# K tiles loaded further ahead of V tiles, and the gate folded into the attention weights, in a one-core decode kernel

## The chip, the core and the metric

The kernel runs on one core of one Trainium2 chip. The metric is the device time of one execution in microseconds (us); 0.2% of it is about 5 us. A core has a matmul engine (TensorE, in the profile PE, with its weight loads PEld), a vector engine (VectorE, DVE), a scalar engine (ScalarE, ACT), GpSimd (POOL) and SyncE (SP), whose queue issues every DMA of this kernel. A DMA is spread over 16 DMA engines.

## The reference

One token (a row `x` of 512 numbers) passes through attention over a cached K and V of 32 heads, 65,536 positions and 128 numbers per position, and through a small gated feed-forward block; a scalar gate mixes the two. All inputs are bf16.

```python
def reference(A_x, A_k_cache, A_v_cache, A_wq, A_wo, B_x, B_w_gate, B_w_up, B_w_down, gate_w):
    x = A_x
    g = sigmoid((x * gate_w).sum(-1, keepdims=True))      # one scalar
    q = (x @ A_wq).reshape(1, 1, 32, 128)                 # heads moved ahead of positions
    scores = einsum("bhqd,bhkd->bhqk", q, A_k_cache) * (128 ** -0.5)
    p = softmax(scores, axis=-1)
    o = einsum("bhqk,bhkd->bhqd", p, A_v_cache)
    a = o.reshape(1, 1, 4096) @ A_wo
    b = (silu(x @ B_w_gate) * (x @ B_w_up)) @ B_w_down
    return g * a + (1 - g) * b
```

K and V are 512 MB each, so nearly all bytes that the kernel reads (1,087.64 MB by the profile) are these two.

## The kernel before

**Tiles.** A tile of K or V holds 16,384 positions: 128 partitions of 128 positions, 4 MB. A head has G = 4 tiles of each, so N = 128 tiles of K and 128 of V. They share one ring of five buffers of 4 MB (`SLOTS`, line 17; pool `ring`); the weights `wq_t`, `gu_t` and `wd_t` pass through the same ring at the start. A load that needs a buffer waits on SP's queue until the last reader of an old tile is done, and all later loads wait behind it, since that queue is in order.

**A K tile** (`products`, line 197, and `scores`, line 216). DVE multiplies the tile by the query, copied to all partitions (line 207), and then folds 128 numbers per position down to 16 with three adds of halves (line 211). PE sums the last 16 with an identity matrix in 16 accumulated matmuls (line 221) into the head's score tile `S_ps` in PSUM. The K buffer is free after those.

**A V tile** (`values`, line 252). PE makes 32 matmuls, four positions of each partition at a time: `P_sb` (the exponentials) is the weight, V the moving operand, and a 4 x 512 tile `O_ps` accumulates over a head (line 258). The V buffer is free after those. The diagonal blocks of `O_ps` add up to the head's output.

**Between the two**, once per head: DVE takes the row maximum of the scores (`row_max`, line 230); ACT spreads it on a diagonal (line 235); PE makes it visible to all partitions (line 237); DVE takes the maximum over that (`top`, line 242); ACT makes the exponentials and their row sums (line 246). After the head's last V tile, `head_out` (line 267) copies `O_ps` to SBUF on ACT, PE sums the row sums over partitions (line 271) and collects the four diagonal blocks (line 275); `project` (line 284) takes the reciprocal of the sum, multiplies the head's output by it on DVE (lines 286 and 287) and adds its part of the output projection to `a_ps` (line 288), with rows of A_wo that `load_wo` (line 138) brings in for four heads at a time.

**Order.** Each engine runs its instructions in the order in which the program issues them. The loop at line 296 runs n over 132 steps. Step n loads K tile n and V tile n - 4, so that V runs four tiles behind K. In a step that begins a head, DVE's work on the K tile is cut into two halves, and the row maximum, `top` and the reciprocal of earlier heads are woven between the halves (lines 306 to 315). The feed-forward block is worked in steps 1 to 3. After the loop comes the last head's `head_out` and `project`, then `diff` = a - b (line 332), `out_sb` = diff * g + b (line 334) and the store (line 338).

Of the kernel before, what the change touches and what calls it, by code (L numbers as in the profile page):

```python
# [8 lines left out]
ACT = mybir.ActivationFunctionType  # L9
ALU = mybir.AluOpType  # L10
AXIS = mybir.AxisListType
P = 128
# [3 lines left out]
NB = 128  # L16
SLOTS = 5

WIDTH = 16


@with_exitstack
def kernel(
# [14 lines left out]
    nc = tc.nc  # L38
    bf16 = mybir.dt.bfloat16
    f32 = mybir.dt.float32  # L40

    _, H, Sk, Dh = A_k_cache.shape
    D = A_x.shape[2]
# [3 lines left out]
    G = Sk // (NB * P)  # L47
    NBH = Sk // P
    N = H * G
    QG = 4  # L50
    assert Dh == P and Sk % (NB * P) == 0 and NBH <= 512 and H % QG == 0 and G >= 2
    scale = float(Dh) ** -0.5

    consts = ctx.enter_context(tc.tile_pool(name="consts", bufs=1))
    ring = ctx.enter_context(tc.tile_pool(name="ring", bufs=SLOTS))
    small = ctx.enter_context(tc.tile_pool(name="small", bufs=2))
    wo_pool = ctx.enter_context(tc.tile_pool(name="wo_pool", bufs=2))
    psum_s = ctx.enter_context(tc.tile_pool(name="psum_s", bufs=2, space=bass.MemoryType.PSUM))
    psum_o = ctx.enter_context(tc.tile_pool(name="psum_o", bufs=2, space=bass.MemoryType.PSUM))
    psum_a = ctx.enter_context(tc.tile_pool(name="psum_a", bufs=1, space=bass.MemoryType.PSUM))  # L60
    psum_m = ctx.enter_context(tc.tile_pool(name="psum_m", bufs=2, space=bass.MemoryType.PSUM))
# [20 lines left out]
    ones_f = consts.tile([P, P], f32, name="ones_f")  # L82
# [6 lines left out]

    rowsum = consts.tile([P, H], f32, name="rowsum")  # L90
    oT = consts.tile([P, H], bf16, name="oT")
    gval = consts.tile([1, 1], f32, name="gval")
    b_sb = consts.tile([1, D], f32, name="b_sb")
    a_ps = psum_a.tile([1, D], f32, name="a_ps")

    K_tiles, V_tiles, S_tiles, P_tiles, O_tiles = {}, {}, {}, {}, {}
# [38 lines left out]
    WG = 4  # L135
    wo_tiles = {}

    def load_wo(g):
        wo_tiles[g] = wo_pool.tile([P, WG, D], bf16, name="wo_sb")
        rows = A_wo[g * WG * P : (g + 1) * WG * P, :]  # L140
        nc.sync.dma_start(out=wo_tiles[g], in_=rows.rearrange("(h p) n -> p h n", p=P))
# [20 lines left out]
        nc.scalar.activation(out=eg, in_=gu_sb[:, :FT], func=ACT.Exp, scale=-1.0)  # L162
        return gu_sb, eg

    def feed_forward_out(gu_sb, eg):
        nc.vector.tensor_scalar_add(eg, eg, 1.0)
        nc.vector.reciprocal(eg, eg)
        hprod = consts.tile([P, FT], f32, name="hprod")
        nc.vector.tensor_tensor(out=hprod, in0=gu_sb[:, :FT], in1=eg, op=ALU.mult)
        hT = consts.tile([P, FT], bf16, name="hT")  # L170
        nc.vector.tensor_tensor(out=hT, in0=hprod, in1=gu_sb[:, FT:], op=ALU.mult)
        xg = consts.tile([P, KT], f32, name="xg")
        nc.vector.tensor_tensor(out=xg, in0=xT, in1=gwT, op=ALU.mult)
        xs = consts.tile([P, 1], f32, name="xs")
        nc.vector.tensor_reduce(out=xs, in_=xg, axis=AXIS.X, op=ALU.add)
        b_ps = psum_m.tile([1, D], f32, name="b_ps", tag="misc")
        for ft in range(FT):
            nc.tensor.matmul(
                b_ps,
                lhsT=hT[:, ft : ft + 1],  # L180
                rhs=wd_sb[:, ft, :],
                start=(ft == 0),
                stop=(ft == FT - 1),
            )
        nc.scalar.activation(out=b_sb, in_=b_ps, func=ACT.Copy)
        g_ps = psum_m.tile([1, 1], f32, name="g_ps", tag="misc")
        nc.tensor.matmul(g_ps, lhsT=xs, rhs=ones_f[:, 0:1], start=True, stop=True)
        eg2 = consts.tile([1, 1], f32, name="eg2")
        nc.scalar.activation(out=eg2, in_=g_ps, func=ACT.Exp, scale=-1.0)
        return eg2  # L190

    def gate(eg2):
        nc.vector.tensor_scalar_add(eg2, eg2, 1.0)
        nc.vector.reciprocal(gval, eg2)


    def products(n, a, b):

        h = n // G
        K = K_tiles[n][:, a:b, :]  # L200
        qb = q_bc[:, h * Dh : (h + 1) * Dh]
        q_rep = bass.AP(
            tensor=qb.tensor,
            offset=qb.offset,
            ap=[list(qb.ap[0]), [0, b - a], [1, Dh]],
        )
        yield nc.vector.tensor_tensor(out=K, in0=K, in1=q_rep, op=ALU.mult)  # L207
        half = Dh
        while half > WIDTH:
            half //= 2  # L210
            yield nc.vector.tensor_tensor(  # L211
                out=K[:, :, 0:half], in0=K[:, :, 0:half], in1=K[:, :, half : 2 * half],
                op=ALU.add,
            )
# [15 lines left out]
    def row_max(h):  # L230

        m = small.tile([P, 1], f32, name="m")
        nc.vector.tensor_reduce(out=m, in_=S_tiles[h], axis=AXIS.X, op=ALU.max)  # L233
        diag = small.tile([P, P], f32, name="diag")
        nc.scalar.activation(out=diag, in_=ident_f, func=ACT.Copy, scale=m)  # L235
        mT_ps = psum_m.tile([P, P], f32, name="mT_ps", tag="misc")
        nc.tensor.matmul(mT_ps, lhsT=ones_f, rhs=diag, start=True, stop=True)  # L237
        return mT_ps

    def exponentials(h, mT_ps):  # L240
        top = small.tile([P, 1], f32, name="top")
        nc.vector.tensor_reduce(out=top, in_=mT_ps, axis=AXIS.X, op=ALU.max)  # L242
        bias = small.tile([P, 1], f32, name="bias")
        nc.scalar.activation(out=bias, in_=top, func=ACT.Copy, scale=-scale)  # L244
        P_tiles[h] = small.tile([P, NBH], bf16, name="P_sb")
        nc.scalar.activation(  # L246
            out=P_tiles[h], in_=S_tiles[h], func=ACT.Exp, bias=bias, scale=scale,
            accum_out=rowsum[:, h : h + 1],
        )
        del S_tiles[h]  # L250

    def values(n):

# [10 lines left out]
            )  # L264
        del V_tiles[n]

    def head_out(h):
        O_sb = small.tile([4, 4 * Dh], f32, name="O_sb")
        nc.scalar.activation(out=O_sb, in_=O_tiles.pop(h), func=ACT.Copy)  # L269
        oh_ps = psum_m.tile([P, 2], f32, name="oh_ps", tag="misc")  # L270
        nc.tensor.matmul(  # L271
            oh_ps[:, 1:2], lhsT=ones_f, rhs=rowsum[:, h : h + 1], start=True, stop=True
        )
        for c in range(4):
            nc.tensor.matmul(  # L275
                oh_ps[:, 0:1],
                lhsT=O_sb[:, c * Dh : (c + 1) * Dh],
                rhs=ident_f[0:4, c : c + 1],
                start=(c == 0),
                stop=(c == 3),  # L280
            )
        return oh_ps

    def project(h, oh_ps):
        recip = small.tile([P, 1], f32, name="recip")
        nc.vector.reciprocal(recip, oh_ps[:, 1:2])  # L286
        nc.vector.tensor_tensor(out=oT[:, h : h + 1], in0=oh_ps[:, 0:1], in1=recip, op=ALU.mult)  # L287
        nc.tensor.matmul(  # L288
            a_ps,
            lhsT=oT[:, h : h + 1],  # L290
            rhs=wo_tiles[h // WG][:, h % WG, :],
            start=(h == 0), stop=(h == H - 1),
        )

    ff = None
    for n in range(N + G):
        h, g = divmod(n, G)
        v = n - G
        if g == 0 and h % WG == 2 and h // WG + 1 < H // WG:
            load_wo(h // WG + 1)  # L300
        if n < N and n > 1:
            load(K_tiles, A_k_cache, n, "K_t")
        if v >= 0:
            load(V_tiles, A_v_cache, v, "V_t", (0, NB) if v < N - 1 else (0, 64, 96, 112, NB))
        vector = products(n, 0, NB) if n < N else iter(())
        if g == 0 and h > 0:
            if n < N:
                vector = (i for a in (0, NB // 2) for i in products(n, a, a + NB // 2))
            next(vector, None)
            mT_ps = row_max(h - 1)  # L310
            next(vector, None)
            exponentials(h - 1, mT_ps)
            if h > 1:
                oh_ps = head_out(h - 2)
                next(vector, None)
                project(h - 2, oh_ps)
        if n == 1:
            ff = feed_forward_in()
        if n == 2:
            ff = feed_forward_out(*ff)  # L320
        if n == 3:
            gate(ff)
        for _ in vector:
            pass
        if v >= 0:
            values(v)
        if n < N:
            scores(n)
    project(H - 1, head_out(H - 1))

    diff = consts.tile([1, D], f32, name="diff")
    nc.vector.tensor_tensor(out=diff, in0=a_ps, in1=b_sb, op=ALU.subtract)  # L332
    out_sb = consts.tile([1, D], bf16, name="out_sb")
    nc.vector.scalar_tensor_tensor(  # L334
        out=out_sb, in0=diff, scalar=gval[0:1, 0:1], in1=b_sb,
        op0=ALU.mult, op1=ALU.add,
    )
    nc.sync.dma_start(out=out[0], in_=out_sb)


# [28 lines left out]
```

## Time and profile before

| what | value |
|---|---|
| median of 3 runs (lowest to highest) | 2556.45 us (2555.84 to 2557.48) |
| the profiled execution's own time | 2556.5 us |
| its span, first to last instruction | 2554.7 us |
| bytes moved, mean rate over the span | 1088.61 MB, 426 GB/s |
| DMA engines, share of the span (main queue) | 99.2% |
| DVE busy | 2173.4 us (85%) |
| PE busy, weight loads beside it | 1738.5 us (68%), 717.3 us (28%) |
| ACT busy | 66.8 us (3%) |
| mean granted TensorE clock (1 is full speed) | 0.754 |

The profile takes one execution apart. "Busy" is the time in which an engine executes; "idle before" in a group's or a timeline's line is how long the engine sat before the instruction, with what released it behind an arrow. The granted clock is the share of full speed that TensorE was allowed at the time. The time of the run is 1.8 us above the span; that part lies around the instructions, and I carry it over unchanged.

### The profile page before, as it was taken

The page shows a single profiled execution, that of the slowest core. Times are in us where ns is not written, and L with a number is a line of the kernel's source. Part 1 is how long each engine was busy: PE and PEld are TensorE (multiplying, and loading weights), DVE is VectorE, ACT ScalarE, POOL GpSimd, SP SyncE. Part 2 cuts the span into 40 slices and gives each one's busy share as a digit, 9 for nine tenths or more (in the row PEclk, how much of TensorE's full clock was granted, in tenths as well). Part 3 has the DMA queues.
Part 4 walks back from the last instruction along what each step waited for, and adds up shares of the span by engine and source line. Part 5 has one row for each costly group of instructions (what it writes and reads, how often), then busy time and mean ns, then how long its engine had stood idle before and what let it go on. Part 6 is the DMA issues. An engine that isn't in the chain of part 4 may idle for free.

```text
span 2554.7 us, 15161 instructions
## 1 busy us (share of the span) xinstructions
PE 1738.5 (68%) x6720; PEld 717.3 (28%) x6720; DVE 2173.4 (85%) x779; ACT 66.8 (3%) x174; POOL 0.7 (0%) x6
## 2 busy tenths in 40 slices
PE   3477666766776676667666776677666667766677
PEld 2232222322232222222222232222222222322233
DVE  6998888888988888888888888888888888888982
ACT  1000000000000000000000000000000000000000
POOL 0000000000000000000000000000000000000000
PEclk7677777777777777777777777777777777777778
DMA  9999999999999999999999999999999999999996
GB/s 407 434 426 433 430 431 430 429 432 430 432 429 431 429 432 429 430 431 429 432 429 431 428 433 429 432 428 433 429 431 431 428 432 430 431 430 432 430 431 278
DMA packets 42451, 1088.61 MB, mean 426 GB/s; under 512 B 4625, under 2 KB 8722, under 8 KB 8978
## 3 DMA queue, kind: packets, MB, share of 16 engines
q1 hardware_dynamic: 42386, 1087.66, 99.2%
q8 instruction: 52, 0.85, 0.1%
q14 instruction: 13, 0.11, 0.0%
HBM read 1087.64 MB, written 0.00 MB: 426 GB/s over the span
## 4 chain that ended last, share of the span: by engine, by line
DMA 72%; PE 24%; DVE 3%; issue 0%; ACT 0%; SPq 0%; DVEq 0%
DMA V_t<-in_A_v_cache_dram 70%; PE O_ps L258 23%; DVE K_t L207 2%; DVE K_t L211 1%; DMA K_t<-in_A_k_cache_dram 1%; DMA wq_t<-in_A_wq_dram 0%; PE qg_ps L113 0%; PE S_ps L221 0%; PE oh_ps L275 0%; DVE m L233 0%; ACT O_sb L269 0%; PE a_ps L288 0%; ACT P_sb L246 0%; DVE out_sb L334 0%; DVE diff L332 0%
## 5 line engine op out<-in xcount | busy, mean ns | idle before, releaser
L258 PE MATMUL O_ps<-V_t,P_sb 128*4 128x512 bf16 x4096 | 1157.0, 452 | 544.1 <-DMA V_t<-in_A_v_cache_dram 541.9
L207 DVE TENSOR_TENSOR K_t<-K_t,q_bc 128x16384 bf16<-128x16384 bf16 (+1 forms) x159 | 1116.9, 7025 | 249.3 <-DMA K_t<-in_A_k_cache_dram 243.8
L211 DVE TENSOR_TENSOR K_t<-K_t 128x2048 bf16<-128x2048 bf16 (+3 forms) x477 | 1030.0, 2159 | 13.2
L258 PEld LDWEIGHTS <-P_sb 128*4 128x4 bf16 x4096 | 397.3, 97 | 1298.0 <-issue 955.1
L221 PE MATMUL S_ps<-K_t,ident_b 128*128 128x128 bf16 x2048 | 466.0, 394 | 71.0 <-DVE K_t L211 61.3
L221 PEld LDWEIGHTS <-ident_b 128*128 128x128 bf16 x2048 | 223.1, 114 | 308.1 <-issue 110.2
L275 PE MATMUL oh_ps<-ident_f,O_sb 4*128 4x1 f32 x256 | 58.8, 346 | 76.5 <-ACT O_sb L269 76.5
L286 DVE RECIPROCAL recip<-oh_ps 128x1 f32<-128x1 f32 x32 | 5.4, 168 | 105.1 <-PE oh_ps L275 105.1
L237 PE MATMUL mT_ps<-diag,ones_f 128*128 128x128 f32 x64 | 24.9, 490 | 92.3 <-ACT diag L235 92.3
L275 PEld LDWEIGHTS oh_ps<-ident_f,O_sb 4*128 4x128 f32 x256 | 56.1, 319 | 79.2 <-ACT O_sb L269 76.6
L235 ACT ACTIVATE diag<-ident_f,m 128x128 f32<-128x128 f32 x32 | 12.9, 402 | 2327.3 <-DVE m L233 2327.3
L237 PEld LDWEIGHTS mT_ps<-diag,ones_f 128*128 128x128 f32 x64 | 15.6, 304 | 108.0 <-ACT diag L235 108.0
L288 PE MATMUL a_ps<-wo_sb,oT 128*1 128x512 bf16 x32 | 18.5, 580 | 14.6 <-DVE oT L287 14.6
L233 DVE TENSOR_REDUCE m<-S_ps 128x1 f32<-128x512 f32 x32 | 21.8, 683 | 6.5 <-PE S_ps L221 6.5
L246 ACT ACTIVATE P_sb<-S_ps,bias 128x512 bf16<-128x512 f32 x32 | 22.0, 687 | 1.0
L269 ACT ACTIVATE O_sb<-O_ps 4x512 f32<-4x512 f32 x32 | 18.2, 570 | 32.0 <-PE O_ps L258 32.0
L113 PE MATMUL qg_ps<-wq_t,X_bc 128*128 128x512 bf16 x32 | 8.4, 428 | 14.1 <-DMA wq_t<-in_A_wq_dram 14.1
L271 PEld LDWEIGHTS oh_ps<-rowsum,ones_f 128*128 128x128 f32 x64 | 16.8, 321 | 0.4 <-issue 0.4
L271 PE MATMUL oh_ps<-rowsum,ones_f 128*128 128x1 f32 x64 | 13.3, 278 | 0.0
L242 DVE TENSOR_REDUCE top<-mT_ps 128x1 f32<-128x128 f32 x32 | 9.0, 282 | 1.0 <-PE mT_ps L237 1.0
L113 PEld LDWEIGHTS <-X_bc 128*128 128x128 bf16 x32 | 3.5, 108 | 18.5 <-issue 13.0
L244 ACT ACTIVATE bias<-top 128x1 f32<-128x1 f32 x32 | 6.5, 203 | 62.8 <-DVE top L242 62.8
(34 smaller groups left out, 46.3 us busy)
## 6 DMA issues: line engine op xcount, KB each, us to landing
K_t<-in_A_k_cache_dram SPq DMA_DIRECT2D x128, 4096.0 KB, 35.5
V_t<-in_A_v_cache_dram SPq DMA_DIRECT2D x127, 4096.0 KB, 29.4
wq_t<-in_A_wq_dram SPq DMA_DIRECT2D x1, 4096.0 KB, 12.4
wo_sb<-in_A_wo_dram SPq DMA_DIRECT2D x8, 512.0 KB, 30.1
V_t<-in_A_v_cache_dram SPq DMA_DIRECT2D x1, 2048.0 KB, 24.4
gu_t<-in_B_w_gate_dram SPq DMA_DIRECT2D x1, 1792.0 KB, 34.7
gu_t<-in_B_w_up_dram SPq DMA_DIRECT2D x1, 1792.0 KB, 38.4
wd_t<-in_B_w_down_dram SPq DMA_DIRECT2D x1, 1792.0 KB, 42.2
```

Source lines behind the costliest of these rows:

```text
L207: yield nc.vector.tensor_tensor(out=K, in0=K, in1=q_rep, op=ALU.mult)
L211: yield nc.vector.tensor_tensor(out=K[:, :, 0:half], in0=K[:, :, 0:half], in1=K[:, :, half : 2 * half], op=ALU.add,)
L221: nc.tensor.matmul(S_tiles[h][:, g * NB : (g + 1) * NB], lhsT=ident_b, rhs=K_tiles[n][:, :, c], start=(c == 0), stop=(c == WIDTH - 1),)
L233: nc.vector.tensor_reduce(out=m, in_=S_tiles[h], axis=AXIS.X, op=ALU.max)
L235: nc.scalar.activation(out=diag, in_=ident_f, func=ACT.Copy, scale=m)
L237: nc.tensor.matmul(mT_ps, lhsT=ones_f, rhs=diag, start=True, stop=True)
L246: nc.scalar.activation(out=P_tiles[h], in_=S_tiles[h], func=ACT.Exp, bias=bias, scale=scale, accum_out=rowsum[:, h : h + 1],)
L258: nc.tensor.matmul(O_tiles[h], lhsT=P_tiles[h][:, g * NB + j : g * NB + j + 4], rhs=V_tiles[n][:, j : j + 4, :], start=(g == 0 and j == 0) ...
L269: nc.scalar.activation(out=O_sb, in_=O_tiles.pop(h), func=ACT.Copy)
L271: nc.tensor.matmul(oh_ps[:, 1:2], lhsT=ones_f, rhs=rowsum[:, h : h + 1], start=True, stop=True)
L275: nc.tensor.matmul(oh_ps[:, 0:1], lhsT=O_sb[:, c * Dh : (c + 1) * Dh], rhs=ident_f[0:4, c : c + 1], start=(c == 0), stop=(c == 3),)
L288: nc.tensor.matmul(a_ps, lhsT=oT[:, h : h + 1], rhs=wo_tiles[h // WG][:, h % WG, :], start=(h == 0), stop=(h == H - 1),)
```

## The change

It does five things.

1. The loop runs over a list of steps. V starts at step 5 instead of 4, so K is five tiles ahead. From step 40 on, each step with n % 4 == 3 loads no V while V is less than eight tiles behind; that happens at n = 43, 47 and 51, after which K is eight tiles ahead. After the last K come eight steps with V alone (before: four).
2. `products` is issued whole in every step. The row maximum follows it on DVE. The rest of the softmax (`spread`, `exponentials`, and a new `total`) is issued after the step's `values` and `scores`. `P_sb` has a pool of its own with three buffers instead of two.
3. The sum of the row sums over partitions moves from `head_out` to `total`, right behind the exponentials. Two steps into the next head, `weight` on DVE makes gate / sum, one factor per head (`rg`). `head_out` then scales with that factor on ACT.
4. The gate is computed on all partitions. (1 - gate) * b is made in step 3 and opens the accumulation in `a_ps` with a matmul against a single 1, so the end is one copy from `a_ps` to `out_sb`. The feed-forward's middle part now comes behind `products(2)` on DVE instead of ahead of it.
5. In the last `head_out`, ACT and DVE each copy one half of `O_ps`. `load_wo` goes by V's tile number: with V tiles 8, 24, 40, ... .

```diff
+LAG = 8
+SPREAD = 40
+    ppool = ctx.enter_context(tc.tile_pool(name="ppool", bufs=3))
...
-    def feed_forward_out(gu_sb, eg):
+    def feed_forward_mid(gu_sb, eg):
...
-        nc.scalar.activation(out=b_sb, in_=b_ps, func=ACT.Copy)
-        g_ps = psum_m.tile([1, 1], f32, name="g_ps", tag="misc")
-        nc.tensor.matmul(g_ps, lhsT=xs, rhs=ones_f[:, 0:1], start=True, stop=True)
+        g_ps = psum_m.tile([P, 1], f32, name="g_ps", tag="misc")
+        nc.tensor.matmul(g_ps, lhsT=ones_f, rhs=xs, start=True, stop=True)
...
+    def feed_forward_out(b_ps, eg2):
         nc.vector.tensor_scalar_add(eg2, eg2, 1.0)
         nc.vector.reciprocal(gval, eg2)
+        rest = consts.tile([1, 1], f32, name="rest")
+        nc.vector.tensor_scalar(
+            out=rest, in0=gval[0:1, :], scalar1=-1.0, scalar2=1.0, op0=ALU.mult, op1=ALU.add
+        )
+        nc.scalar.activation(out=b_sb, in_=b_ps, func=ACT.Copy, scale=rest)
+        nc.tensor.matmul(a_ps, lhsT=ones_f[0:1, 0:1], rhs=b_sb, start=True, stop=False)
...
+    def total(h):
+        tot_ps = psum_m.tile([P, 1], f32, name="tot_ps", tag="misc")
+        nc.tensor.matmul(tot_ps, lhsT=ones_f, rhs=rowsum[:, h : h + 1], start=True, stop=True)
+        return tot_ps
+
+    def weight(h, tot_ps):
+        recip = small.tile([P, 1], f32, name="recip")
+        nc.vector.reciprocal(recip, tot_ps)
+        nc.vector.tensor_tensor(out=rg[:, h : h + 1], in0=recip, in1=gval, op=ALU.mult)
...
-    def head_out(h):
+    def head_out(h, last=False):
         O_sb = small.tile([4, 4 * Dh], f32, name="O_sb")
-        nc.scalar.activation(out=O_sb, in_=O_tiles.pop(h), func=ACT.Copy)
...
+        cut = 2 * Dh if last else 4 * Dh
+        nc.scalar.activation(out=O_sb[:, :cut], in_=O_ps[:, :cut], func=ACT.Copy)
+        if last:
+            nc.vector.tensor_copy(out=O_sb[:, cut:], in_=O_ps[:, cut:])
...
-        nc.vector.reciprocal(recip, oh_ps[:, 1:2])
-        nc.vector.tensor_tensor(out=oT[:, h : h + 1], in0=oh_ps[:, 0:1], in1=recip, op=ALU.mult)
+        nc.scalar.activation(
+            out=oT[:, h : h + 1], in_=oh_ps, func=ACT.Copy, scale=rg[:, h : h + 1]
+        )
...
+    steps = []
+    v = 0
+    for n in range(N):
+        due = n > G and not (n >= SPREAD and n % 4 == 3 and n - v < LAG)
+        steps.append((n, v if due else None))
+        v += due
+    while v < N:
+        steps.append((None, v))
+        v += 1
...
+    for n, v in steps:
+        if n is not None and n > 1:
             load(K_tiles, A_k_cache, n, "K_t")
+        if v is not None:
+            if v % (WG * G) == 2 * G and v // (WG * G) + 1 < H // WG:
+                load_wo(v // (WG * G) + 1)
             load(V_tiles, A_v_cache, v, "V_t", (0, NB) if v < N - 1 else (0, 64, 96, 112, NB))
+        if n is not None:
+            products(n)
+            if n % G == 0 and n > 0:
+                diag = row_max(n // G - 1)
+            if n % G == 2 and n > G:
+                weight(n // G - 1, tot_ps)
+        elif S_tiles:
+            diag = row_max(H - 1)
         if n == 1:
             ff = feed_forward_in()
         if n == 2:
-            ff = feed_forward_out(*ff)
+            ff = feed_forward_mid(*ff)
         if n == 3:
-            gate(ff)
+            feed_forward_out(*ff)
+        if done is not None:
+            head_out(done)
+        if v is not None:
             values(v)
+        if n is not None:
             scores(n)
+        if diag is not None:
+            h = (n if n is not None else N) // G - 1
+            exponentials(h, spread(diag))
+            tot_ps = total(h)
+            diag = None
+            if n is None:
+                weight(h, tot_ps)
+        if done is not None:
+            project(done)
+        done = v // G if v is not None and v % G == G - 1 else None
+    head_out(H - 1, last=True)
+    project(H - 1)
-    diff = consts.tile([1, D], f32, name="diff")
-    nc.vector.tensor_tensor(out=diff, in0=a_ps, in1=b_sb, op=ALU.subtract)
     out_sb = consts.tile([1, D], bf16, name="out_sb")
-    nc.vector.scalar_tensor_tensor(
-        out=out_sb, in0=diff, scalar=gval[0:1, 0:1], in1=b_sb,
-        op0=ALU.mult, op1=ALU.add,
-    )
+    nc.vector.tensor_copy(out=out_sb, in_=a_ps)
```

More of the change, by code (lines that the diff above doesn't have):

```diff
@@ L91 @@
     oT = consts.tile([P, H], bf16, name="oT")
-    gval = consts.tile([1, 1], f32, name="gval")
+    gval = consts.tile([P, 1], f32, name="gval")
+    rg = consts.tile([P, H], f32, name="rg")
     b_sb = consts.tile([1, D], f32, name="b_sb")
@@ L184, in feed_forward_out, with products @@
             )
-        nc.scalar.activation(out=b_sb, in_=b_ps, func=ACT.Copy)
-        g_ps = psum_m.tile([1, 1], f32, name="g_ps", tag="misc")
-        nc.tensor.matmul(g_ps, lhsT=xs, rhs=ones_f[:, 0:1], start=True, stop=True)
-        eg2 = consts.tile([1, 1], f32, name="eg2")
+        g_ps = psum_m.tile([P, 1], f32, name="g_ps", tag="misc")
+        nc.tensor.matmul(g_ps, lhsT=ones_f, rhs=xs, start=True, stop=True)
+        eg2 = consts.tile([P, 1], f32, name="eg2")
         nc.scalar.activation(out=eg2, in_=g_ps, func=ACT.Exp, scale=-1.0)
-        return eg2
-    def gate(eg2):
+        return b_ps, eg2
+    def feed_forward_out(b_ps, eg2):
         nc.vector.tensor_scalar_add(eg2, eg2, 1.0)
         nc.vector.reciprocal(gval, eg2)
-    def products(n, a, b):
+        rest = consts.tile([1, 1], f32, name="rest")
[4 more added lines that the diff above has]
+        nc.tensor.matmul(a_ps, lhsT=ones_f[0:1, 0:1], rhs=b_sb, start=True, stop=False)
+    def products(n):
         h = n // G
-        K = K_tiles[n][:, a:b, :]
+        K = K_tiles[n]
         qb = q_bc[:, h * Dh : (h + 1) * Dh]
@@ L204, in products @@
             offset=qb.offset,
-            ap=[list(qb.ap[0]), [0, b - a], [1, Dh]],
+            ap=[list(qb.ap[0]), [0, NB], [1, Dh]],
         )
-        yield nc.vector.tensor_tensor(out=K, in0=K, in1=q_rep, op=ALU.mult)
+        nc.vector.tensor_tensor(out=K, in0=K, in1=q_rep, op=ALU.mult)
         half = Dh
@@ L210, in products @@
             half //= 2
-            yield nc.vector.tensor_tensor(
+            nc.vector.tensor_tensor(
                 out=K[:, :, 0:half], in0=K[:, :, 0:half], in1=K[:, :, half : 2 * half],
@@ L235, in row_max, with spread @@
         nc.scalar.activation(out=diag, in_=ident_f, func=ACT.Copy, scale=m)
+        return diag
+    def spread(diag):
         mT_ps = psum_m.tile([P, P], f32, name="mT_ps", tag="misc")
@@ L244, in exponentials @@
         nc.scalar.activation(out=bias, in_=top, func=ACT.Copy, scale=-scale)
-        P_tiles[h] = small.tile([P, NBH], bf16, name="P_sb")
+        P_tiles[h] = ppool.tile([P, NBH], bf16, name="P_sb")
         nc.scalar.activation(
@@ L265, in values @@
         del V_tiles[n]
-    def head_out(h):
+    def head_out(h, last=False):
         O_sb = small.tile([4, 4 * Dh], f32, name="O_sb")
[L269 to L272, printed above, removed]
-        )
+        O_ps = O_tiles.pop(h)
+        cut = 2 * Dh if last else 4 * Dh
+        nc.scalar.activation(out=O_sb[:, :cut], in_=O_ps[:, :cut], func=ACT.Copy)
+        if last:
+            nc.vector.tensor_copy(out=O_sb[:, cut:], in_=O_ps[:, cut:])
+        oh_ps = psum_m.tile([P, 1], f32, name="oh_ps", tag="misc")
         for c in range(4):
             nc.tensor.matmul(
-                oh_ps[:, 0:1],
+                oh_ps,
                 lhsT=O_sb[:, c * Dh : (c + 1) * Dh],
@@ L281, in head_out, with project @@
             )
[L282 to L287, printed above, removed]
+        nc.scalar.activation(
+            out=oT[:, h : h + 1], in_=oh_ps, func=ACT.Copy, scale=rg[:, h : h + 1]
+        )
+    def project(h):
         nc.tensor.matmul(
@@ L291, in project @@
             rhs=wo_tiles[h // WG][:, h % WG, :],
-            start=(h == 0), stop=(h == H - 1),
-        )
[L295 to L301, printed above, removed]
+            start=False,
+            stop=(h == H - 1),
+        )
+    steps = []
[7 more added lines that the diff above has]
+        v += 1
+    ff = done = diag = tot_ps = None
+    for n, v in steps:
+        if n is not None and n > 1:
             load(K_tiles, A_k_cache, n, "K_t")
-        if v >= 0:
+        if v is not None:
+            if v % (WG * G) == 2 * G and v // (WG * G) + 1 < H // WG:
+                load_wo(v // (WG * G) + 1)
             load(V_tiles, A_v_cache, v, "V_t", (0, NB) if v < N - 1 else (0, 64, 96, 112, NB))
[L305 to L316, printed above, removed]
+        if n is not None:
[6 more added lines that the diff above has]
+            diag = row_max(H - 1)
         if n == 1:
@@ L319 @@
         if n == 2:
-            ff = feed_forward_out(*ff)
+            ff = feed_forward_mid(*ff)
         if n == 3:
-            gate(ff)
-        for _ in vector:
-            pass
-        if v >= 0:
+            feed_forward_out(*ff)
+        if done is not None:
+            head_out(done)
+        if v is not None:
             values(v)
-        if n < N:
+        if n is not None:
             scores(n)
-    project(H - 1, head_out(H - 1))
-    diff = consts.tile([1, D], f32, name="diff")
-    nc.vector.tensor_tensor(out=diff, in0=a_ps, in1=b_sb, op=ALU.subtract)
+        if diag is not None:
[10 more added lines that the diff above has]
+    project(H - 1)
     out_sb = consts.tile([1, D], bf16, name="out_sb")
-    nc.vector.scalar_tensor_tensor(
-        out=out_sb, in0=diff, scalar=gval[0:1, 0:1], in1=b_sb,
-        op0=ALU.mult, op1=ALU.add,
-    )
+    nc.vector.tensor_copy(out=out_sb, in_=a_ps)
     nc.sync.dma_start(out=out[0], in_=out_sb)
```

## The prediction

> **What bounds the kernel.** I read the page's slices first, then SP's waits, then the tail and the opening in the timeline and in narrow windows.
>
> ```profile
> GB/s 407 434 426 433 430 431 430 429 432 430 432 429 431 429 432 429 430 431 429 432 429 431 428 433 429 432 428 433 429 431 431 428 432 430 431 430 432 430 431 278
> ```
>
> The loads run at 428 to 434 GB/s in every slice between the first and the last: no head boundary and no wait of DVE or PE dents them. So the loads bound the kernel, and only the ends can give anything: the first slice's 407 and the last one's 278. SP's waits say why there is no dent:
>
> ```profile
> SPq L104 <- PE O_ps L258: 1196.0, 124, 14.3
> SPq L104 <- PE S_ps L221: 407.4, 127, 3.7
> ```
>
> Some 124 loads wait for `values` and 127 for `scores`: V takes a V's buffer, K takes a K's, in the order in which buffers fall free.
>
> The tail:
>
> ```profile
> 2479.98 9.34 PE L258 MATMUL O_ps<-V_t,P_sb 128*4 128x512 bf16 x32 [7.04 <-DMA V_t<-in_A_v_cache_dram]
> 2498.49 8.01 DVE L211 TENSOR_TENSOR K_t<-K_t 128x8192 bf16<-128x8192 bf16 x3
> 2499.42 9.85 PE L258 MATMUL O_ps<-V_t,P_sb 128*4 128x512 bf16 x32 [6.53 <-DMA V_t<-in_A_v_cache_dram]
> ...
> 2519.22 29.25 PE L258 MATMUL O_ps<-V_t,P_sb 128*4 128x512 bf16 x128
> 2548.50 0.59 ACT L269 ACTIVATE O_sb<-O_ps 4x512 f32<-4x512 f32 x1 [32.04 <-PE O_ps L258]
> 2550.22 0.17 DVE L286 RECIPROCAL recip<-oh_ps 128x1 f32<-128x1 f32 x1 [31.44 <-PE oh_ps L275]
> 2550.64 0.38 PE L288 MATMUL a_ps<-wo_sb,oT 128*1 128x512 bf16 x1 [0.46 <-DVE oT L287]
> 2551.06 0.68 DVE L332 TENSOR_TENSOR diff<-a_ps,b_sb 1x512 f32<-1x512 f32 x1 [0.47 <-PE a_ps L288]
> 2551.77 0.74 DVE L334 SCALAR_TENSOR_TENSOR out_sb<-diff,gval,b_sb 1x512 bf16<-1x512 f32 x1
> 2552.54 0.32 SPq L338 DMA_DIRECT2D out_dram<-out_sb  x1
> ```
>
> Two V landings lie 19.44 us apart with one K between, so a 4 MB tile takes 9.72 us. At the end PE works off 128 matmuls in one stretch to 2548.47, at the pace of PE. Windows (PE, PEld, DVE, ACT, POOL busy, granted clock, DMA share, GB/s) show the last bytes before 2539.0:
>
> ```profile
> 2514.00:2516.00 2.00, 0.61 (x4) 0.52 (x4) 0.29 (x1) 1.07 (x5) 0.00 (x0) 0.83 1.07 459
> 2516.00:2518.00 2.00, 1.49 (x7) 1.49 (x8) 0.00 (x0) 0.46 (x1) 0.00 (x0) 0.50 0.78 336
> ...
> 2538.00:2539.00 1.00, 1.00 (x6) 0.36 (x5) 0.00 (x0) 0.00 (x0) 0.00 (x0) 1.00 0.02 8
> 2539.00:2540.00 1.00, 1.00 (x6) 0.42 (x5) 0.00 (x0) 0.00 (x0) 0.00 (x0) 1.00 0.00 0
> ```
>
> The span ends 15.7 us after the loads (2554.7 - 2539.0). That is all the change can take from. The bytes are the same, so with no pause added the loads still end at 2539.0.
>
> **Part by part. The tail (parts 1, 4, 5).** With K eight ahead, the last K lands 8 x 9.72 = 77.8 us before the end. DVE needs 8.69 + 8.01 = 16.70 us for it, PE's `values`, `scores` and the softmax chain some 15 more, so the last P is ready about 45 us before V's last tile; the wait for it is gone. PE then follows V. What is late next is V's last two tiles: V126 lands 9.7 us before the end, V127 in four cuts. The 128 matmuls above took 29.25 us, the later ones 0.2175 us each at full clock (26.1 us for the last 120). At full clock V126 ends 9.7 - 32 x 0.2175 = 2.7 us before the last landing, V127's first half has come by then, and its 32 matmuls take 7.0 more: PE ends 4.2 us after the loads. If V126 starts at half clock it takes the 9.4 us of the rows above: PE ends 6.6 us after. Which one depends on a PE gap of 9.72 - 6.96 = 2.8 us. A gap of 6.5 to 7 us costs the clock every time; the 2514 to 2518 windows show it fall to 0.50 though PE had worked 0.61 us of 2. I take the middle, 5.4, with both ends in the range.
>
> The Trainium skill ("TensorE: Matmul & The Clock Gate", Part 1) has the gate close after an idle window of about 3.4 us; by that rule 2.8 us keeps the clock and the term would be 4.2, while the window at 2514 speaks for 6.6.
>
> Behind PE there were 2554.7 - 2548.47 = 6.2 us. `O_sb` in two halves beside each other: between the 0.40 us of ACT's 128x128 copies and 0.59, I take 0.45, saves 0.14. The reciprocal and product (2550.22 to 2550.64) become one ACT operation, about the 0.20 us of `bias` plus a hand-over of 0.05: saves 0.17. `diff` and the mix (2551.06 to 2552.54) become one copy like `diff`: saves 0.75. That leaves 5.15.
>
> **The middle (parts 1 to 3).** The question is whether DVE and PE still free the buffers in time. Per head the loads take 8 x 9.72 = 77.8 us. DVE: 4 x 16.70, maximum 0.68, `weight` 0.17 + 0.16, and the wait for `top`. Behind DVE in that wait stands the next K's `products`. `top` now follows `values` and `scores` on PE: unhurried, V lands 9.72 after K, `values` 9.4, `scores` 3.64, `spread` 0.80, `top` 0.29, so DVE is free 23.9 us after the K landed, 4.4 past the next landing; hurried, 4.7 us after `products`. Together 72.5 us, 5.3 spare. Before, the halves cost 4.42 and 4.28 twice, 0.7 us more per head. A step without V gives DVE two K tiles 9.72 apart: 7.0 us of backlog, three times, one head apart: 7.0, 8.7, 10.4, and then it melts. A K load waits for the K three back, free 22.9 us after landing; it must be issued 9.72 + 2.7 us before it should land (2.7 is from the opening below), 45.9 us after that landing, or 36.2 next to a skipped V. 22.9 is then at most 31 with the backlog: 5 us of cover remain. Cost: nothing, hidden by the queued loads; without that cover, each us costs one. `total` (two passes, 0.4 us), `project` and `head_out` on PE lie in its gaps of 6.5 us. `P_sb`'s third buffer covers V's longer lag. A_wo's eight loads keep size and count and come up to four steps later, over 200 us before use: nothing on SP's queue.
>
> **The opening (parts 2 and 4).** Here the queue runs thin.
>
> ```profile
> 58.70 8.69 DVE L207 TENSOR_TENSOR K_t<-K_t,q_bc 128x16384 bf16<-128x16384 bf16 x1 [0.43 <-DMA K_t<-in_A_k_cache_dram]
> 100.77 9.40 PE L258 MATMUL O_ps<-V_t,P_sb 128*4 128x512 bf16 x32 [2.21 <-ACT P_sb L246]
> ...
> wq_t<-in_A_wq_dram SPq DMA_DIRECT2D x1, 4096.0 KB, 12.4
> ```
>
> K2 lands at 58.70. Then come K3, K4, K5, V0, K6, V1, K7, V2, so without a pause V2 lands at 58.70 + 8 x 9.72 = 136.5. V2 takes V0's buffer and waits for `values(0)`. DVE: `products(2)` 58.7 to 75.4, the feed-forward's six operations (1.13 before) to 76.5, `products(3)` to 93.2, gate to 93.6, `products(4)` to 110.3. The row maximum, now behind that product, to 111.0; `scores(4)` on PE ends at 114.1, `spread` 114.9, `top` 115.2, bias and exponentials 116.4, `total` 116.8, `values(0)` (9.40) 126.2. Issued then, V2 lands no sooner than 126.2 + 12.4 = 138.6, the 12.4 being the lone load's row: 2.1 us of pause. K8 behind it waits for `scores(5)` at about 135.9: 135.9 + 12.4 = 148.3, just within 138.6 + 9.72. `wd_t`'s buffer, freed at 81.4 instead of 65.9, is V0's, issued in time (81.4 + 12.4 against 97.6). I take 2.1; bounds 0 (`values(0)` at 7.07 us, as at 113.80 with a full clock) and 3.5 (`total` and the opening matmul twice as dear). The opening matmul (f32, 512 columns), which no row shows, costs between 0 and four times `spread`'s 0.80 us for 128 columns, 3.2 us; it stands ahead of `scores(3)` on PE. Gate and copy are ready at 94.2, so `scores(3)` ends by 94.2 + 3.2 + 3.64 = 101.0 and V1, issued then, has 101.0 + 12.4 = 113.4 against its 117.0: nothing, at either bound. K7 waits for `scores(4)`: 114.1 + 12.4 = 126.5 against 126.7, just in time. The wider gate tiles have one column as before: nothing.
>
> **Sum.** Loads end 2539.0 + 2.1 = 2541.1, PE + 5.4 = 2546.5, end + 5.15 = 2551.65, plus the 1.8 around the span: 2553.4; I say 2553.2. The profiled execution took 2556.5, the median 2556.45: no correction.
>
> **Rivals.** A, *the opening doesn't pause and the clock holds*: 2539.0 + 0 + 4.2 + 5.15 + 1.8 = 2550.2, and less with a run's scatter of 0.7. For it: the clock was full at `values(1)` in the opening, so `values(0)` may be quick too. Against: the clock row. 26%. B, *nothing gained*: each V tile at 9.85 us, longer than its landing of 9.72, PE still behind at the end, about 9.9 us after the loads: 2539.0 + 2.1 + 9.9 + 5.15 + 1.8 = 2558.0. Against: in the 29.25 us stretch PE was at 0.2175 us a matmul, 7.0 us a tile, after its first eight matmuls; work without gaps gets the full clock within one tile. 8%. C, *slower*: in the opening, buffers pass in strict rotation, V2 then waiting for `scores(5)`: issued at 135.9, landing 148.3, a pause of 11.8 instead of 2.1: 2563.0. It makes a loss beyond 0.2% from a pause of 10.4 us on or so (5.3 us gained without it, plus 5.1). Against: SP's two rows above. 8%. My forecast: 58%.
>
> **The numbers.** A measurement tells some 0.2%, 5.1 us, from no change: faster is below 2551.3, slower above 2561.6. Range 2549.0 to 2557.0: below, A with scatter; above, 6.6 and 3.5 at once. Faster: A and the forecast's lower edge, 0.30; slower 0.07; same 0.63.
>
> **What would show it.** Right: loads end near 2541, PE's last stretch ends 4 to 7 us behind them, the last slice moves clearly more than 278 GB/s; one dent in the loads near 130 us, none at 830 to 1000. Wrong: dents at head boundaries or at steps 43, 47 and 51, a last stretch of over 64 matmuls in one piece, or DVE waits for `top` beyond 10 us.

## The result, and the profile after

The changed kernel takes 2647.11 us (median of 6 runs, 2646.06 to 2649.95) against 2556.24 us before in the same comparison: a ratio of 1.0356 (95% interval 1.0343 to 1.0369). It is 91 us slower; I had forecast 2553.2 with a range to 2557.0. The profiled execution has a span of 2644.3 us.

The rate of the loads, in 40 slices of the span, on the page of the changed kernel:

```profile
GB/s 408 416 427 431 431 431 431 431 429 432 430 432 431 429 433 430 426 403 433 400 397 389 397 432 399 399 389 397 428 402 396 391 399 428 397 397 391 426 405 295
```

For sixteen slices the line reads as before, but for a little at the start. The seventeenth has 426, and from the eighteenth on most have 389 to 405. A slice is 66 us, so the break lies between 1060 and 1120 us: behind the third step without V (n = 51), from which on K is eight tiles ahead. Windows over these stretches (PE, PEld, DVE, ACT, POOL busy, granted clock, DMA share, GB/s) give the size:

```profile
0.00:830.00 830.00, 538.54 (x2152) 228.01 (x2153) 723.91 (x223) 28.05 (x72) 0.70 (x6) 0.74 1.00 428
830.00:1054.00 224.00, 140.79 (x552) 60.39 (x551) 209.76 (x65) 5.85 (x16) 0.00 (x0) 0.71 1.00 430
1054.00:2530.00 1476.00, 932.99 (x3618) 391.32 (x3617) 1183.34 (x352) 38.16 (x108) 0.00 (x0) 0.72 0.95 404
```

The first 830 us (five tiles ahead) and the steps in which the distance grows run at full rate. The 1,476 us behind them run at 404 instead of 430 GB/s: 1476 x 26 / 430 = 89 us, and the span grew by 2644.3 - 2554.7 = 89.6. That the two agree so closely is partly chance: the loads themselves end 87 us later (before 2626 against 2539.0), and the rest of the growth lies in the tail, which comes further down. But neither the new opening nor the steps without V cost it; something does that returns with every head at a distance of eight.

The four longest waits of PE and DVE in the changed kernel (engine, line, waited for: us in total, times, longest) name it:

```profile
PE S_ps L232 <- DVE K_t L222: 436.5, 87, 17.5
DVE top L256 <- PE mT_ps L251: 352.1, 32, 16.4
PE oh_ps L301 <- ACT O_sb L296: 264.3, 21, 14.5
PE O_ps L283 <- DMA V_t<-in_A_v_cache_dram: 147.5, 28, 7.8
```

The kernel before, in the same form for PE, and its group of `top` (busy us, mean ns | idle before):

```profile
PE O_ps L258 <- DMA V_t<-in_A_v_cache_dram: 541.9, 90, 8.6
L242 DVE TENSOR_REDUCE top<-mT_ps 128x1 f32<-128x128 f32 x32 | 9.0, 282 | 1.0 <-PE mT_ps L237 1.0
```

Before, PE waited 541.9 us for V's loads; now 147.5, and it waits for DVE and for ACT. DVE waited 1.0 us in all for `top`; now it waits 352.1 us, 11 us per head and up to 16.4. In the first 800 us it is 44.1 us for 10 heads, 4.4 each; from 1060 us on it is 284.7 us for 18, 15.8 each. One head of the second kind in order of time (start, duration, engine, line; in brackets the idle time before and its releaser; weight loads are left out here and in the timelines below):

```profile
1894.77 1.89 PE L283 MATMUL O_ps<-V_t,P_sb 128*4 128x512 bf16 x8
...
1909.23 8.01 DVE L222 TENSOR_TENSOR K_t<-K_t 128x8192 bf16<-128x8192 bf16 x3
1917.16 0.68 DVE L244 TENSOR_REDUCE m<-S_ps 128x1 f32<-128x512 f32 x1
1917.88 0.40 ACT L246 ACTIVATE diag<-ident_f,m 128x128 f32<-128x128 f32 x1 [66.44 <-DVE m L244]
1918.18 0.57 ACT L296 ACTIVATE O_sb<-O_ps 4x512 f32<-4x512 f32 x1
1918.81 1.86 PE L301 MATMUL oh_ps<-ident_f,O_sb 4*128 4x1 f32 x8 [14.52 <-ACT O_sb L296]
1920.60 9.79 PE L283 MATMUL O_ps<-V_t,P_sb 128*4 128x512 bf16 x32
...
1930.32 3.63 PE L232 MATMUL S_ps<-K_t,ident_b 128*128 128x128 bf16 x16
...
1933.77 0.40 PE L251 MATMUL mT_ps<-diag,ones_f 128*128 128x128 f32 x2
...
1934.28 0.29 DVE L256 TENSOR_REDUCE top<-mT_ps 128x1 f32<-128x128 f32 x1 [16.43 <-PE mT_ps L251]
...
2503.09 0.68 DVE L244 TENSOR_REDUCE m<-S_ps 128x1 f32<-128x512 f32 x1
```

Read it from ACT. The head's last `values` ends at 1896.66 (1894.77 + 1.89), so `O_sb` (line 296) could run then. It runs at 1918.18, because `diag` (line 246) stands ahead of it on ACT, and `diag` waits for the row maximum, which waits for DVE's whole product of this step. PE is in order too: the finished head's `oh_ps` waits for `O_sb`, and behind it stand the step's `values`, `scores` and `spread`, for which `top` waits, and behind `top` stands DVE's next product. So DVE, after its row maximum at 1917.84, waits 16.43 us, of which `oh_ps` (1.86) and the V tile (9.79) are work that PE could have done while DVE was multiplying: the V tile, whose load was issued at 1879.85 and landed 20.4 us later, lay ready. (The Trainium skill, "TensorE: Matmul & The Clock Gate", Architectural detail, says of ACT and DVE that they are "strict FIFO"; `O_sb` starting behind `diag`, 21.5 us after its input was ready, agrees.)

Why only at a distance of eight: a head's last V tile is one with v % 4 == 3. At a distance of five it falls in a step with n % 4 == 0, and `head_out` in the next one. At eight it falls in n % 4 == 3, and `head_out` in n % 4 == 0, the step of the row maximum. The first such step is n = 56 (V tile 47 is loaded at n = 55), the last n = 124: 18 heads.

From the row maximum at 1917.16 to that at 2503.09 there are seven heads: 83.70 us per head. DVE's sum is 4 x 16.70 + 0.68 + 0.33 + 15.8 = 83.6 us. Loads need 77.8 for K and V alone. DVE has become the bound.

### The profile page after: what moved, and what is told of

Its sections match the earlier page's. It is cut to its first block, busy times and chain, and to the rows that moved or that the text cites. A ratio compares the mean times of both kernels' runs of the same rounds, so it can differ in the third digit from the quotient of the medians.

```text
span 2644.3 us, 15002 instructions
## 1 busy us (share of the span) xinstructions
PE 1706.2 (65%) x6722; PEld 718.4 (27%) x6722; DVE 2158.7 (82%) x656; ACT 75.7 (3%) x206; POOL 0.7 (0%) x6
## 4 chain that ended last, share of the span: by engine, by line
DVE 60%; PE 19%; DMA 18%; issue 2%; ACT 1%; SPq 0%; DVEq 0%
DVE K_t L218 32%; DVE K_t L222 27%; DMA V_t<-in_A_v_cache_dram 15%; PE O_ps L283 13%; PE S_ps L232 4%; DMA K_t<-in_A_k_cache_dram 3%; PE oh_ps L301 1%; DVE m L244 0%; DMA wq_t<-in_A_wq_dram 0%; ACT O_sb L296 0%; PE qg_ps L118 0%; ACT diag L246 0%; PE mT_ps L251 0%; DVE top L256 0%; DVE rg L275 0%
## 5 line engine op out<-in xcount | busy, mean ns | idle before, releaser
L283 PE MATMUL O_ps<-V_t,P_sb 128*4 128x512 bf16 x4096 | 1136.0, 447 | 147.5 <-DMA V_t<-in_A_v_cache_dram 147.5
L218 DVE TENSOR_TENSOR K_t<-K_t,q_bc 128x16384 bf16<-128x16384 bf16 x128 | 1111.7, 8685 | 57.0 <-DMA K_t<-in_A_k_cache_dram 56.9
L222 DVE TENSOR_TENSOR K_t<-K_t 128x8192 bf16<-128x8192 bf16 (+2 forms) x384 | 1016.4, 2647 | 13.2
L283 PEld LDWEIGHTS <-P_sb 128*4 128x4 bf16 x4096 | 387.5, 96 | 870.0 <-issue 514.2
L232 PEld LDWEIGHTS <-ident_b 128*128 128x128 bf16 x2048 | 236.1, 117 | 665.4 <-issue 465.7
L256 DVE TENSOR_REDUCE top<-mT_ps 128x1 f32<-128x128 f32 x32 | 9.3, 292 | 352.1 <-PE mT_ps L251 352.1
L301 PE MATMUL oh_ps<-ident_f,O_sb 4*128 4x1 f32 x256 | 57.6, 342 | 264.4 <-ACT O_sb L296 264.3
L269 PE MATMUL tot_ps<-rowsum,ones_f 128*128 128x1 f32 x64 | 16.5, 327 | 47.0 <-ACT P_sb L260 47.0
L269 PEld LDWEIGHTS tot_ps<-rowsum,ones_f 128*128 128x128 f32 x64 | 13.8, 269 | 53.7 <-ACT P_sb L260 53.7
L296 ACT ACTIVATE O_sb<-O_ps 4x512 f32<-4x512 f32 (+1 forms) x32 | 18.1, 565 | 86.7 <-PE O_ps L283 86.7
L251 PE MATMUL mT_ps<-diag,ones_f 128*128 128x128 f32 x64 | 14.1, 305 | 0.0
```

What stands on the lines that cost most here:

```text
L222: nc.vector.tensor_tensor(out=K[:, :, 0:half], in0=K[:, :, 0:half], in1=K[:, :, half : 2 * half], op=ALU.add,)
L232: nc.tensor.matmul(S_tiles[h][:, g * NB : (g + 1) * NB], lhsT=ident_b, rhs=K_tiles[n][:, :, c], start=(c == 0), stop=(c == WIDTH - 1),)
L269: nc.tensor.matmul(tot_ps, lhsT=ones_f, rhs=rowsum[:, h : h + 1], start=True, stop=True)
L283: nc.tensor.matmul(O_tiles[h], lhsT=P_tiles[h][:, g * NB + j : g * NB + j + 4], rhs=V_tiles[n][:, j : j + 4, :], start=(g == 0 and j == 0) ...
L296: nc.scalar.activation(out=O_sb[:, :cut], in_=O_ps[:, :cut], func=ACT.Copy)
L301: nc.tensor.matmul(oh_ps, lhsT=O_sb[:, c * Dh : (c + 1) * Dh], rhs=ident_f[0:4, c : c + 1], start=(c == 0), stop=(c == 3),)
```

## The experiments

Three theories. **A**: the meeting of `diag` and `O_sb` in one step on ACT's queue. **B**: the distance itself: five buffers are too few for K eight tiles ahead, or the backlog from the steps without V never melts. **C**: the late softmax, `spread` behind `values` and `scores`, is dear at any distance. Times are medians; ratios are to the kernel before.

**1. `head_out` ahead of the row maximum, LAG 8.** PE, DVE and SP keep their order; on ACT, `O_sb` and `oT` stand ahead of `diag`.

```diff
+        if done is not None:
+            head_out(done)
         if n is not None:
             products(n)
...
-        if done is not None:
-            head_out(done)
         if v is not None:
             values(v)
```

> The changed kernel with one thing moved: a finished head's `head_out` is issued ahead of the step's `products` and row maximum. Only ACT's order differs (`O_sb` and `oT` ahead of `diag` in the steps n % 4 == 0); PE, DVE and SP have the same order as in the changed kernel. Theory A, the queue on ACT: at a lag of eight the finished head and the row maximum fall in one step, `O_sb` waits on ACT behind `diag`, hence for DVE's `products`, and PE's `values`, `scores` and `spread`, for which DVE's `top` waits, stand behind it; with the order turned, `top` waits 4 to 5 us per head instead of 15.8, the loads run at 430 GB/s to the end, and the time is 2550 to 2556 us. Theory B, the distance itself: five buffers are too few for K eight tiles ahead, DVE's backlog from the three steps without V never melts; the time stays at 2640 to 2650. Theory C, the late softmax: `spread` behind `values` and `scores` is dear at every head; the time stays above 2620.

Measured: 2551.9 us, ratio 0.9983 (0.9974 to 0.9991). The same kind of step in its timeline:

```profile
1835.29 10.02 PE L283 MATMUL O_ps<-V_t,P_sb 128*4 128x512 bf16 x32 [6.36 <-DMA V_t<-in_A_v_cache_dram]
...
1845.35 0.59 ACT L296 ACTIVATE O_sb<-O_ps 4x512 f32<-4x512 f32 x1 [54.71 <-PE O_ps L283]
1848.80 1.86 PE L301 MATMUL oh_ps<-ident_f,O_sb 4*128 4x1 f32 x8
...
1856.22 9.80 PE L283 MATMUL O_ps<-V_t,P_sb 128*4 128x512 bf16 x32 [5.55 <-DMA V_t<-in_A_v_cache_dram]
1861.76 0.69 DVE L244 TENSOR_REDUCE m<-S_ps 128x1 f32<-128x512 f32 x1
1862.48 0.40 ACT L246 ACTIVATE diag<-ident_f,m 128x128 f32<-128x128 f32 x1 [11.51 <-DVE m L244]
...
1869.84 0.29 DVE L256 TENSOR_REDUCE top<-mT_ps 128x1 f32<-128x128 f32 x1 [7.40 <-PE mT_ps L251]
```

`O_sb` now runs at 1845.35, as soon as its input is ready, PE begins the next V tile when it lands (1856.22), 5.5 us before the row maximum, and the loads run at 428 to 434 GB/s from the fourth slice to the last but one. The rate line of the page, and DVE's wait for `top` over 18 heads of that stretch (us in total, times), first in the changed kernel, then here:

```profile
GB/s 407 418 419 429 432 430 432 431 428 430 433 429 434 428 432 431 431 431 430 431 430 432 430 429 432 431 431 432 429 430 431 432 431 430 431 431 430 432 431 311
```

```profile
  PE mT_ps L251: 284.7, 18
```

```profile
  PE mT_ps L251: 102.0, 18
```

`top` waits 5.7 us per head (4 to 5 were expected) in place of 15.8. From the first of these `top` to the last, 17 heads, it is 78.2 us per head here (1087.1 to 2416.6) and 83.6 in the changed kernel (1098.5 to 2519.1): 5.4 us of loss for each. Turning the order of two operations on ACT gives back 95 us, at the same distance and with the same late softmax: A holds, and B and C fall as causes of the loss.

**2. LAG 9.** One number.

```diff
-LAG = 8
+LAG = 9
```

> The changed kernel with LAG = 9 (K nine tiles ahead, one more step without V), nothing else. Theory A: a head's last V tile now falls in a step n % 4 == 0 and its `head_out` in the next step, with n % 4 == 1, away from the row maximum; from step 60 on no stall, only the heads met while the lag was eight (one or two) lose some 6 us each: 2552 to 2566 us. Theory B: further ahead is worse: 2650 us or more. Theory C: as the changed kernel, 2640 to 2650.

Measured: 2551.3 us, ratio 0.9981 (0.9971 to 0.9990), `top` waiting 79.1 us over 15 heads, 5.3 each, and 156.2 us over the whole run. Further ahead is as fast as 1. The time lies under the expectation, which had one or two heads lose while the distance was eight. That was miscounted: with LAG 9 step 55 loads no V either, V tile 47 comes at n = 56 and its `head_out` at n = 57, so no head at all meets a row maximum.

**3. LAG 5.** No step without V.

```diff
-LAG = 8
+LAG = 5
```

> The changed kernel with LAG = 5: no step without V, K stays five tiles ahead to the end. Theory A: `head_out` falls in steps n % 4 == 1, so no stall; the loads end near 2541 and PE some 5 us behind them: 2551 to 2557 us, with `top` waiting 4.4 us per head as in the changed kernel up to step 43. Theory B: the same, 2551 to 2557, so this run doesn't part A from B. Theory C: above 2620.

Measured: 2552.01 us, ratio 0.9983 (0.9974 to 0.9991), `top` waiting 168.6 us over all 32 heads, 5.3 each (4.4 were expected). The line of experiment 2, then that of experiment 3:

```profile
DVE top L256 <- PE mT_ps L251: 156.2, 32, 6.7
```

```profile
DVE top L256 <- PE mT_ps L251: 168.6, 32, 6.7
```

Five, eight (in order) and nine tiles ahead can't be told apart: beyond five the distance brings nothing that these runs can tell.

**4. `spread` first, LAG 8.** `diag` stays ahead of `O_sb`; the chain is cut at its other link.

```diff
+        if diag is not None:
+            h = (n if n is not None else N) // G - 1
+            exponentials(h, spread(diag))
         if v is not None:
             values(v)
...
         if diag is not None:
-            h = (n if n is not None else N) // G - 1
-            exponentials(h, spread(diag))
             tot_ps = total(h)
```

> The changed kernel (LAG 8, `diag` still ahead of `O_sb` on ACT) with `spread` and the exponentials issued ahead of `values` and `scores` instead of behind them. It cuts the other link of the chain: PE still waits for DVE's product before a finished head's `oh_ps` and the V tile behind it, but `top` no longer waits for `values` and `scores`: diag 0.4, O_sb 0.57, oh 1.86, spread 0.6, so 3.5 to 4 us per head. Theory A: DVE is back under the loads' 77.8 us per head and the loss goes, 2550 to 2562 us (the upper part if `values`, still held up by some 14 us once per head, frees V's buffers too late). Theory B: 2640 or more. Theory C: 2550 to 2562, so A and C part in the first run only.

Measured: 2556.16 us, ratio 0.9997 (0.9988 to 1.0006). PE still waits for the finished head, but DVE no longer pays:

```profile
PE oh_ps L301 <- ACT O_sb L296: 283.4, 21, 17.1
DVE top L256 <- PE mT_ps L251: 86.4, 32, 3.7
```

PE's wait for `O_sb` is as long as in the changed kernel (283.4 against 264.3 us), `top`'s is a quarter (86.4 against 352.1), and 91 us are back. So the loss came through DVE's wait, not through PE's. Most of the 4 us that remain against experiment 1 lie in the opening, where PE now holds V's buffer up at step 8:

```profile
180.00:190.00 10.00, 9.43 (x38) 3.69 (x38) 8.68 (x3) 1.91 (x5) 0.00 (x0) 0.83 0.52 223
```

At 223 GB/s for 10 us, (430 - 223) x 10 / 430 = 4.8 us of loads are missing there; the same window of experiment 1 has 439. Taken over the third slice of the page, 64 us long, the rate is 395 GB/s against 419 in experiment 1: 64 x 24 / 430 = 3.6 us net.

**5. The reverse test: LAG 5, each `head_out` held back.** K is five tiles ahead, no step is without V, and a finished head waits for the next step n % 4 == 0, where it again stands behind `diag`.

```diff
-LAG = 8
+LAG = 5
...
-    ff = done = diag = tot_ps = None
+    ff = held = diag = tot_ps = None
...
-        if done is not None:
-            head_out(done)
+        due = held is not None and (n is None or n % G == 0)
+        if due:
+            head_out(held)
...
-        if done is not None:
-            project(done)
-        done = v // G if v is not None and v % G == G - 1 else None
+        if due:
+            project(held)
+            held = None
+        if v is not None and v % G == G - 1:
+            held = v // G
```

> The reverse test: the LAG 5 kernel, K five tiles ahead to the end and no step without V, with each finished head's `head_out` and `project` held back to the next step n % 4 == 0, there behind the row maximum on ACT. Theory A (the meeting of `diag` and `O_sb` in one step, whatever the distance): every head from step 12 to step 124, 29 of them, loses what the changed kernel lost, 83.7 - 77.8 = 5.9 us: 2552 + 171 = 2723 us, 2690 to 2750, with `top` waiting 15 to 16.4 us per head. Theory B (the distance): 2551 to 2557, as the LAG 5 kernel.

Measured: 2716.71 us, ratio 1.0631 (1.0616 to 1.0645).

```profile
DVE top L256 <- PE mT_ps L251: 480.6, 32, 16.9
PE oh_ps L301 <- ACT O_sb L296: 423.5, 31, 14.6
```

The meeting alone makes the loss at a distance of five, too: 2716.7 - 2552.0 = 164.7 us over 29 heads, 5.7 each, against the 5.9 expected. The changed kernel against experiment 1 gives 95.2 us over 18 heads, 5.3 each. So the price of A is between 5 and 6 us per head, measured at two distances.

**6 and 7. V tile 126 in two halves**, on experiment 1 and on LAG 9: the tail's next term.

```diff
-            load(V_tiles, A_v_cache, v, "V_t", (0, NB) if v < N - 1 else (0, 64, 96, 112, NB))
+            cuts = {N - 2: (0, 64, NB), N - 1: (0, 64, 96, 112, NB)}
+            load(V_tiles, A_v_cache, v, "V_t", cuts.get(v, (0, NB)))
```

> The first experiment's kernel (LAG 8, `head_out` first) with V tile 126 also loaded in two halves, so that PE can begin it half a tile earlier. By the tail's sum PE then ends about 1.3 us behind the last landing (last cut's 4 matmuls and a rest of the cut before) instead of 4 to 7: 2.5 to 5 us less than the first experiment, 2547 to 2550 us. Rival: the loads' ragged end (the rate falls from 430 to 200 GB/s over the last 12 us) already lets the slowest engine set everything, or the extra descriptors cost as much: 2551 to 2553.

> The LAG 9 kernel with the same cut of V tile 126. PE's gap before that tile, which decides whether the clock is lost, shrinks from 2.7 us: 2547 to 2550 us by the tail's sum, 2551 to 2553 by its rival.

Measured: 2549.71 us, ratio 0.9973 (0.9962 to 0.9984), and 2549.93 us, ratio 0.9974 (0.9965 to 0.9983). Both lie in the upper half of the tail's sum, 2.2 and 1.4 us under their parents; the intervals of parents and cuts overlap, and the kernel before was 0.34 us faster beside these two (2556.48) than beside their parents (2556.82). So the two runs together speak for a gain of 1 to 2 us without proving it. PE's last stretches, first of experiment 1, then of LAG 9, then of experiment 6, and a window of experiment 1 with the granted clock as the last but two:

```profile
2531.08 15.51 PE L283 MATMUL O_ps<-V_t,P_sb 128*4 128x512 bf16 x64 [2.66 <-DMA V_t<-in_A_v_cache_dram]
```

```profile
2529.81 13.97 PE L283 MATMUL O_ps<-V_t,P_sb 128*4 128x512 bf16 x64 [2.67 <-DMA V_t<-in_A_v_cache_dram]
```

```profile
2519.84 13.97 PE L283 MATMUL O_ps<-V_t,P_sb 128*4 128x512 bf16 x64 [1.09 <-DMA V_t<-in_A_v_cache_dram]
2534.50 7.07 PE L283 MATMUL O_ps<-V_t,P_sb 128*4 128x512 bf16 x32 [0.69 <-DMA V_t<-in_A_v_cache_dram]
```

```profile
2532.00:2534.00 2.00, 2.00 (x6) 0.52 (x5) 0.00 (x0) 0.00 (x0) 0.00 (x0) 0.50 0.53 225
```

Uncut, V126 and V127 are one stretch of 64 matmuls from V126's landing; V127 lands 9.72 us later, so PE ends 5.8 us (15.51 - 9.72) or 4.25 us (13.97 - 9.72) behind the loads. With V126 cut, PE has worked it off before V127's first half lands (2534.50), and ends 2541.57. No bytes come after 2539 in that profile, so PE is still at least 2.5 us behind the loads, not the 1.3 expected. These two have the lowest medians, 0.27% and 0.26% under the kernel before, and can't be told apart.

## Why the prediction was wrong, and where it was right

**The step that failed** is "The middle". It has DVE's wait for `top` as "hurried, 4.7 us after `products`. Together 72.5 us, 5.3 spare", and it puts `total`, `project` and `head_out` away with "lie in its gaps of 6.5 us". I followed PE's order and DVE's, and took `head_out` as work for PE's gaps alone, but did not write down ACT's order. There `head_out`'s first operation stands behind `diag` whenever both fall in one step, and I never asked in which step `head_out` falls as the distance grows from five to eight. The wait was 15.8 us, not 4.7; DVE needed 83.7 us per head, not 72.5; the spare 5.3 became a lack of 5.9 against the loads' 77.8, or 5.4 against the 78.2 per head that experiment 1 shows, 18 times (18 x 5.4 = 97 us, measured 95). Where `head_out` doesn't meet the row maximum, the wait is 5.3 to 5.7 us, near the 4.7. The last paragraph of the prediction even has the sign ("DVE waits for `top` beyond 10 us"), as the mark of being wrong; no rival was built on it. The rival that I made for "slower", strict rotation of the buffers, had the wrong place: V2's load is issued as `values(0)` ends (116.71 + 8.91 = 125.62, issue at 125.66), as the prediction had it. SP's two rows, which I held against that rival, couldn't tell: their counts would be much the same if each K took a V's buffer.

**The rest of the sum held** where that order is turned: experiment 1 takes 2551.9 us against 2553.2.

- The opening: `values(0)` was worked out to end at 126.2 and V2's load to be issued then, with a pause of 2.1 us. In the changed kernel:

```profile
116.71 8.91 PE L283 MATMUL O_ps<-V_t,P_sb 128*4 128x512 bf16 x32
...
125.66 0.33 SPq L109 DMA_DIRECT2D V_t<-in_A_v_cache_dram  x1
```

```profile
120.00:130.00 10.00, 5.63 (x25) 2.09 (x24) 9.93 (x3) 0.00 (x0) 0.00 (x0) 0.98 0.91 367
130.00:140.00 10.00, 8.21 (x33) 3.48 (x33) 9.97 (x3) 0.00 (x0) 0.00 (x0) 0.66 0.97 396
```

  The load is issued at 125.66, and the dent is where it was put: (430 - 367 + 430 - 396) x 10 / 430 = 2.3 us in these two windows, 3.0 over all seven from 100 to 170. What counts is where the loads end: in experiment 1 before 2541 (16 GB/s in the last microsecond), against 2539.0 before and 2541.1 in the sum. A kernel without this pause wasn't tried.
- The steps without V: no dent at 830 to 1054 us, as costed (nothing).
- The tail: PE 4.2 to 6.6 us behind the loads; measured 4.25 (LAG 9) and 5.8 (experiment 1). Neither end was wrong: gaps of 2.67 and 2.66 us before V126 kept the clock in one execution and lost it in the other. The eleven times of experiment 1 fall into two groups, 2550.6 to 2551.9 and 2553.3 to 2553.8, with the profiled one in the upper; that fits, but it isn't shown that the clock parts the groups. In the changed kernel itself the term failed with the middle: PE comes out of the last meeting behind the loads and works 96 matmuls in one piece, a sign of being wrong that the prediction named.

```profile
2618.45 20.73 PE O_ps L283 x96
```

```profile
2622.00:2626.00 4.00, 4.00 (x20) 1.57 (x19) 0.00 (x0) 0.00 (x0) 0.00 (x0) 1.00 0.58 231
2626.00:2627.00 1.00, 1.00 (x7) 0.42 (x5) 0.00 (x0) 0.00 (x0) 0.00 (x0) 1.00 0.00 0
```

  PE ends at 2639.18, 13 us behind the loads in place of 5.4.
- The end: 5.15 us behind PE's last matmul; in experiment 1 it is 2551.7 - 2546.6 = 5.1. One part of it didn't go as thought: the halves of `O_sb` don't run beside each other; DVE's starts at 2547.03, after ACT's (2546.62 and 0.37 long), while PE's `oh_ps` already works on ACT's half from 2547.05. That the sum came out all the same is in part luck.
- The distance: it has no term of its own in the sum, and experiment 3 shows none; what the change gains is there with five tiles.

## What to carry to other kernels

A change of distance in a software pipeline moves the step in which rare work (a head's end) falls; write out every engine's queue for that step, ACT's too, not only those that are busy: an engine with 3% load cost 91 us here, because a half-microsecond copy stood behind an operation that waited for the engine that bounds. When PE's order holds work for DVE behind a finished piece's rest, issue the rest's inputs ahead of anything that waits for DVE. Where loads bound and a stall shows at every n-th step, try one step more of distance first: it is one number, and it tells a meeting in one step, which then goes, from a want of buffers, which then grows (less distance would be faster by either).

## What was not expected of the hardware

TensorE's clock after a gap isn't settled by the gap's length alone: 2.67 us kept it (64 matmuls in 13.97 us), 2.66 us lost it (15.51 us, granted clock 0.50 at 2532 to 2534). The Trainium skill ("TensorE: Matmul & The Clock Gate", Part 1) puts the closing of the gate at an idle window of about 3.4 us that runs freely; that it runs freely would let two like gaps end differently, but 2.66 us is shorter than such a window, so an idle one can't be what closed it here. Nor need the gap be near 2.7 us: the same stretch of the tail, behind the same wait of 0.92 us, ran at full pace in experiment 1 and lost the clock in experiment 6 (7.07 and 8.43 us for 32 matmuls). Where the threshold lies, these runs don't show.

```profile
2511.63 7.07 PE L283 MATMUL O_ps<-V_t,P_sb 128*4 128x512 bf16 x32 [0.92 <-DMA V_t<-in_A_v_cache_dram]
```

```profile
2510.11 8.43 PE L283 MATMUL O_ps<-V_t,P_sb 128*4 128x512 bf16 x32 [0.92 <-DMA V_t<-in_A_v_cache_dram]
```
